# A list-scheduled attention and feed-forward kernel: new transfer figures in its planner and 82 fixed nudges of the steps' priorities

## The chip, the core and the metric

One core of a Trainium2 chip runs the kernel. The metric is device time in microseconds (us) for one execution. The engines are TensorE (PE, with its weight loads as PEld), VectorE (DVE), ScalarE (ACT), GpSimd (POOL) and SyncE (SP), whose queue issues nearly all DMA transfers.

## What is computed

Attention over 4 batches, 8 heads, 768 positions, head size 64, where each query sees the first 4 positions (sinks) and a window of 128; then a low-rank mixing over the sequence and a feed-forward pair with a residual:

```python
scores = scale * np.matmul(q, k.transpose(0, 1, 3, 2))
keep = is_sink | in_window
a = np.exp(scores - max); a = a / (np.sum(a, axis=-1, keepdims=True) + 1e-09)
x = (a @ v) as [batch, 768, 512]
u = x + (x.T @ U @ V).T          # U 768x32, V 32x768
out = u + np.maximum(u @ w_ch1, 0.0) @ w_ch2     # 512 -> 2048 -> 512
```

## The kernel before

**Tiling.** Everything is cut into tiles of 128 partitions. Attention works on a pair of heads at a time: scores of half blocks of 64 queries in 64-row tiles of PE (`scores`, line 760; "tiled" matmuls), a masked minimum on DVE (L773), the exponential on ACT (L776), the scaling by the row sums on POOL, ACT or DVE (L797, L794), transposes on PE (L815), copies with a triangular mask on ACT, DVE and POOL (L821, L823, L826), and the product with the values (L857, tiled). The mixing follows (`mix_half`, `mix_end`, L964 to L1042).

**Feed-forward.** Products are formed in a 32-bit matmul type as three products of high and low parts (hi and lo, "split" by a copy and a subtraction, L622, L623, L629, L631). Batch 0 runs plainly (`ffn`, L1077 to L1099) while the weights arrive: each piece of 64-bit weights is loaded, converted by integer steps (`narrow`, L139 to L147, tiles `nr`, `nt`, `spare`) and split into `w` tiles. The parts, and sums of quarters of them (`prepare`), are written to DRAM tensors `wd` and `ws`. Batches 1 to 3 run jointly (`ffn_joint`) with seven products of half-size blocks in place of eight (L1247), in two rounds of four pairs of blocks each; for every product a piece of 256 KB is loaded again from `wd` or `ws` into a slot of a ring (`w0` to `w5`, later `spare`), and used by 3 or 6 matmuls. The results of the products are added on DVE (L1252).

**What sets the order.** All work between the prelude and the end is first recorded as `Step` objects with an engine (or several possible ones with a cost each), reads, writes and a priority; then `Plan.order` arranges them by a list-scheduling model on the host, and the instructions are issued in that order, engine by engine. `forward` goes through time and always starts the ready step of the lowest priority value, choosing the engine of a step that can go to several; buffers of a ring and the port that DVE and POOL share are part of the model. `backward` derives new priorities from the finished plan; 40 rounds of both are run, and the plan kept whose modelled span plus that of `strained` (the same order replayed with longer steps) is least. For a DMA the model takes the issue on SP, a place in one queue of transfers (`lat`, bytes by `RATE`), and a landing after `LAND`:

```python
            if e == "SP":
                dma = max(dma, t + s.dur + 0.65 if s.dur else dma) + s.lat
                end = dma + LAND + s.slack
```

An SP instruction that waits (for a slot to be free, say) holds every later one in SP's queue. PE works off its instructions strictly in order too, so a matmul whose weights are not there stops it. The steps spoken of below are the loads of `weights` inside `ffn_joint` (recorded by `put`, L637), the masked copies of `transposes` (L821 on DVE or L823 on POOL), the conversion's last step (L146 on DVE or L147 on POOL) and the subtractions `tt` (L629 on DVE or L631 on POOL).

## Time and profile before

| | us |
|---|---|
| median of 3 runs (lowest, highest) | 682.69 (681.12, 688.5) |
| the profiled execution | 681.97 |
| its span, first to last instruction | 680.2 |
| PE busy in it | 651.1 |

The profiled execution's own time is 1.8 us more than its span. The profile is of one execution: a page of sums, and views of the trace behind it (waits by who ended them, the chain of work that ended last, groups of equal instructions, stretches of time). A busy PE includes matmuls that run slowly; its granted clock stands beside it as a share of 2.4 GHz.

### The profile page before, as it was taken

The numbers are of one execution on the slowest core, as the hardware profiler recorded it, in microseconds if no ns is written. First come the engines' busy times: TensorE is split into PE (matmuls) and PEld (weight loads), VectorE is DVE, ScalarE is ACT, GpSimd is POOL, SyncE is SP. The second block draws the span as 40 slices with busy tenths as digits, with TensorE's granted clock in tenths as the row PEclk, the third lists the DMA queues.
The fourth block names the chain that finished last, engine by engine and source line by source line (L and its number), as shares of the span: only waits on it lengthen the run. The fifth ranks groups of instructions, "written<-read, shape, count | busy, mean of one in ns | idle before, by whom it ended". The sixth has DMA issues, their size and how long they took to land.

```text
span 680.2 us, 15557 instructions
## 1 busy us (share of the span) xinstructions
PE 651.1 (96%) x5302; PEld 599.2 (88%) x5302; DVE 535.6 (79%) x1464; ACT 427.8 (63%) x1185; POOL 261.3 (38%) x336
## 2 busy tenths in 40 slices
PE   7898999999989989998999999999999999999997
PEld 5665888888979879988979989899999999999996
DVE  7999999998999878787798799666735964673483
ACT  6986788887774378774478866265437535543551
POOL 4742656357536157555144555112303211020120
PEclk9899999999999999998999999999999999999999
DMA  8569899999769799996899767968887899888882
GB/s 273 187 198 375 302 388 339 363 326 322 259 223 357 235 335 383 359 301 216 274 299 389 261 191 228 318 201 294 264 254 250 264 294 374 249 245 262 250 271 94
DMA packets 111720, 191.57 MB, mean 282 GB/s; under 512 B 10256, under 2 KB 46608, under 8 KB 111632
## 3 DMA queue, kind: packets, MB, share of 16 engines
q1 hardware_dynamic: 111200, 189.90, 83.7%
q8 instruction: 44, 0.72, 0.4%
q10 hardware_dynamic: 432, 0.59, 0.3%
q14 instruction: 44, 0.36, 0.2%
HBM read 141.17 MB, written 49.28 MB: 280 GB/s over the span
## 4 chain that ended last, share of the span: by engine, by line
PE 76%; DVE 10%; DMA 8%; ACT 2%; issue 1%; POOL 0%; SPq 0%; DVEq 0%; POOLq 0%; ACTq 0%
PE bank L1247 48%; PE bank L1099 6%; PE bank L760 4%; PE bank L857 4%; DMA w<-ws 3%; PE bank L815 3%; PE bank L1077 2%; PE bank L1079 2%; PE bank L1078 2%; DMA w<-wd 2%; DVE nt L145 1%; DVE spare L146 1%; DMA ws<-spare 1%; DVE ul L629 1%; PE bank L964 1%
## 5 line engine op out<-in xcount | busy, mean ns | idle before, releaser
L1247 PE MATMUL bank<-w,w 128*128 128x384 f32 x792 | 154.6, 339 | 3.5 <-DVE w L629 1.4
L1247 PEld LDWEIGHTS bank<-w,w 128*128 128x128 f32 x792 | 138.2, 188 | 7.1 <-DVE w L629 1.8
L776 ACT ACTIVATE p<-p,mn 128x132 f32<-128x132 f32 x192 | 75.5, 396 | 20.9 <-DVE mn L773 20.7
L1247 PE MATMUL bank<-w,spare 128*128 128x384 f32 x348 | 67.1, 338 | 0.0
L631 POOL TENSOR_TENSOR w<-uh,w 128x384 fp32r<-128x384 f32 x21 | 22.7, 1081 | 106.9 <-ACT w L622 63.7
L1252 DVE TENSOR_TENSOR big<-bank,big 128x384 f32<-128x384 f32 x84 | 44.6, 551 | 23.5 <-PE bank L1247 23.4
L1247 PEld LDWEIGHTS bank<-w,spare 128*128 128x128 f32 x348 | 61.6, 188 | 0.1
L1099 PE MATMUL bank<-w,hh 128*128 128x512 f32 x192 | 61.4, 401 | 0.0
L773 DVE CUSTOM_DVE_ANT_0 p<-bank,mask 128x132 f32<-128x132 f32 x192 | 48.4, 290 | 0.2
L1077 PE MATMUL bank<-ul,w 128*128 128x384 f32 x128 | 44.3, 346 | 4.3 <-DVE ul L629 1.7
L629 DVE TENSOR_TENSOR spare<-spare 128x128 f32<-128x128 f32 (+1 forms) x93 | 39.0, 444 | 10.1 <-DMA ws<-spare 5.8
L631 POOL TENSOR_TENSOR spare<-spare 128x128 f32<-128x128 f32 (+1 forms) x47 | 30.1, 650 | 42.2 <-DMA ws<-spare 15.8
L1247 PE MATMUL bank<-spare,w 128*128 128x384 f32 x210 | 43.0, 341 | 1.6 <-DMA w<-ws 1.6
L622 ACT CAST w<-ul 128x384 fp32r<-128x384 f32 x56 | 28.8, 514 | 24.2 <-PE bank L1247 19.0
L1079 PE MATMUL bank<-uh,w 128*128 128x384 f32 x128 | 43.1, 336 | 0.0
L1078 PE MATMUL bank<-uh,w 128*128 128x384 f32 x128 | 43.0, 336 | 0.0
L823 POOL TENSOR_SCALAR_AFFINE_SELECT oph<-oph 128x320 f32<-128x320 f32 x51 | 27.3, 548 | 36.3 <-ACT oph L622 35.6
L760 PE MATMUL bank<-kp,qp 64*64 64x196 f32 (+2 forms) x840 | 39.4, 316 | 1.5 <-DMA kp<-in_k_dram 1.3
L1099 PEld LDWEIGHTS bank<-w,hh 128*128 128x128 f32 x192 | 34.5, 188 | 6.8 <-issue 1.4
L797 POOL TENSOR_TENSOR p<-p,r 128x396 f32<-128x396 f32 x32 | 27.9, 879 | 31.4 <-DVE r L786 19.9
L826 POOL TENSOR_SCALAR_AFFINE_SELECT oph<-oph 128x384 f32<-128x384 f32 x64 | 39.6, 639 | 0.1
L1247 PEld LDWEIGHTS bank<-spare,w 128*128 128x128 f32 x210 | 36.8, 188 | 3.2 <-ACT nt L622 1.8
(284 smaller groups left out, 1658.9 us busy)
## 6 DMA issues: line engine op xcount, KB each, us to landing
w<-ws SPq DMA_DIRECT2D x132, 256.0 KB, 4.7
w<-wd SPq DMA_DIRECT2D x102, 256.0 KB, 4.2
big<-in_w_dram SPq DMA_DIRECT2D x32, 512.0 KB, 5.5
ws<-spare SPq DMA_DIRECT2D x32, 512.0 KB, 5.6
spare<-ws SPq DMA_DIRECT2D x60, 256.0 KB, 4.1
wd<-w SPq DMA_DIRECT2D x32, 384.0 KB, 5.7
spare<-wd SPq DMA_DIRECT2D x42, 256.0 KB, 3.9
vp<-in_v_dram SPq DMA_DIRECT2D x15, 384.0 KB, 5.5
```

What stands on the lines that cost most here:

```text
L629: ways = {"DVE": (dve(n), lambda: nc.vector.tensor_tensor(dst(), a(), b(), op), pool)}
L631: ways["POOL"] = (gps(n), lambda: nc.gpsimd.tensor_tensor(dst(), a(), b(), op), True)
L760: nc.tensor.matmul(st()[a * G:(a + 1) * G, x * TW + to:x * TW + to + wd], qr()[at, q0:q0 + G], kr()[at, k0:k0 + wd], start=True, stop=True ...
L773: add("DVE", dve(SW), lambda st=st, x=x, j=j, part=part, at=at: nc.vector.tensor_tensor_reduce(part(), st()[:, x * TW + half * G:x * TW + ...
L776: add("ACT", act(SW) + 0.22, lambda part=part, at=at: nc.scalar.activation(part(), part(), AF.Exp, bias=at(mn), scale=-1.0, accum_out=at(sm)),
L826: add("POOL", 0.126 + CH * 0.914e-3, lambda: nc.gpsimd.affine_select(top(), top(), [[0, NB], [1, G]], ALU.is_ge, 0.0, base=half * G, chann ...
L1077: nc.tensor.matmul(ph()[:, :CH], wh, ul()[:, c, :], start=n == 0, stop=False)
L1078: nc.tensor.matmul(ph()[:, :CH], wl, uh()[:, c, :], start=False, stop=False)
L1079: nc.tensor.matmul(ph()[:, :CH], wh, uh()[:, c, :], start=False, stop=n == NC - 1)
L1099: nc.tensor.matmul(acc[k](), a()[:, sl], w()[:, :, at, m:m + P].rearrange("p d o j -> p o d j"), start=not begin and i == 0 and j == 0, st ...
L1247: nc.tensor.matmul(bank()[:, :CH], w()[:, at:at + P], u()[:, d, :] if n > 1 else u(), start=first and i == 1, stop=last and i == 3 * n, sk ...
L1252: add("DVE", dve(CH), lambda: nc.vector.tensor_tensor(x(), bank()[:, :CH], t(), ALU.add), r=(bank,) if t is x else (bank, t), w=(x,), prio ...
```

## The change

The planner's figures are altered: a transfer lands 2.7 us after its turn in place of 1.3, moves at 360 GB/s in place of 370, and takes 0.1 us from issue to its turn in place of 0.65; issuing costs 0.55 us in place of 0.5; the surcharges on DVE steps, the price of an ACT copy and of one group of transposes are lower. After the 40 rounds, 82 seeds are applied in turn. Each picks a share of the steps, a width and a stretch of the plan, and shifts the priority of a pseudo-random part of the steps that begin there; `forward` then runs once more with the shifted priorities. The seeds are a fixed list, and nothing is tried or judged when the kernel is built. What is computed stays the same.

```diff
-LAND = 1.3
-RATE = 370e3
+LAND = 2.7
+RATE = 360e3
 BEGIN = 1.6
+ISSUE = 0.1
 SLOW = 2.0
-MORE = {"POOL": 0.05, "DVE": 0.01}
-STRAIN = {"POOL": 0.06, "DVE": 0.012, "ACT": 0.008, "SP": 0.02}
+MORE = {"POOL": 0.05, "DVE": 0.005}
+STRAIN = {"POOL": 0.06, "DVE": 0.008, "ACT": 0.008, "SP": 0.02}
+SEED = 30000000
+SHARES = ((0.02, 6), (0.1, 3), (0.5, 1), (0.005, 15))
+LENGTHS = (4, 15, 60, 700)
+MOVES = (
+    14, 21, 30, 36, 138, 157, 184, 202, 227, 304, 404, 569, 588, 647, 815, 1183, 1413, 1473, 1764,
...
+)
@@ order
         self.forward()
+        begin = [s.start for s in self.steps]
+        for move in MOVES:
+            self.nudge(SEED + move, begin)
+        self.forward()
         return sorted(self.steps, key=lambda s: (s.start, s.n))
+
+    def nudge(self, seed, begin):
+        state = (seed * 2654435761 + 12345) % 2 ** 64
+        def draw():
+            nonlocal state
+            state = (state * 6364136223846793005 + 1442695040888963407) % 2 ** 64
+            return (state >> 40) / 16777216.0
+        draw(), draw()
+        share, width = SHARES[int(draw() * 4)]
+        lo = draw() * 680 - 20
+        length = LENGTHS[int(draw() * 4)]
+        share = min(share * (700 / length) ** 0.5, 0.5)
+        for s, t in zip(self.steps, begin):
+            if (lo <= t < lo + length or length == LENGTHS[-1]) and draw() < share:
+                s.prio += (draw() + draw() + draw() - 1.5) * 2 * width
@@ strained, forward
-                dma = max(dma, free[e] + 0.65 if s.dur else dma) + s.lat
+                dma = max(dma, free[e] + ISSUE if s.dur else dma) + s.lat
@@ backward
-                p.ready_b = max(p.ready_b, s.back + p.lat + sync + (1.95 if p.eng == "SP" else 0.0) if whole else s.back - p.dur)
+                p.ready_b = max(p.ready_b, s.back + p.lat + sync + (LAND + 0.65 if p.eng == "SP" else 0.0) if whole else s.back - p.dur)
@@ copy, put, transposes
-        return self.plan.any({"ACT": (act(n) + (0.0 if psum else 0.07), lambda: nc.scalar.copy(dst(), src()), False),
+        return self.plan.any({"ACT": (act(n) + (0.0 if psum else 0.045), lambda: nc.scalar.copy(dst(), src()), False),
-        self.plan.add("SP", 0.5 if rows == P else 0.65, fn, r=r, w=((box, part),) if box else (), lat=nbytes / RATE, prio=prio).slack = slack
+        self.plan.add("SP", 0.55 if rows == P else 0.65, fn, r=r, w=((box, part),) if box else (), lat=nbytes / RATE, prio=prio).slack = slack
-        add("PE", mm(P, NBLK), mms, r=parts + [res], w=(tr,), prio=t0)
+        add("PE", 0.30, mms, r=parts + [res], w=(tr,), prio=t0)
```

Lines of the changed kernel have numbers 34 higher from `copy` on (L1247 is L1281 there, L637 is L671, L629 is L663, L631 is L665) and 12 higher before the planner (L147 is L159).

Place A is on PE, at the end of batch 1's second round of products (about 428 to 434 us in the trace); `w2` is the slot, a read of it by `spare0` is the first of a newly loaded piece. Before:

```order
L1247 MATMUL bank3_184<-w0_862,w2_1056 128x384 x3
L1247 MATMUL bank6_187<-w0_862,w3_1128 128x384 x3
L1247 MATMUL bank6_187<-w1_915,w3_1128 128x384
L1247 MATMUL bank6_187<-w0_862,w3_1128 128x384 x2
L1247 MATMUL bank6_187<-w1_915,w3_1128 128x384 x3
L1247 MATMUL bank4_185<-p2_2922,w4_1218 128x384
L1247 MATMUL bank4_185<-vp2_2884,w4_1218 128x384 x2
L1247 MATMUL bank4_185<-p2_2922,w4_1218 128x384
L1247 MATMUL bank4_185<-vp2_2884,w4_1218 128x384 x2
L1247 MATMUL bank6_187<-w1_915,w3_1128 128x384 x3
L1247 MATMUL bank1_182<-w2_1056,w5_1385 128x384 x6
L1247 MATMUL bank4_185<-spare0_3036,w2_1056 128x384 x6
```

and now, from the last read of the old piece in `w2`:

```order
L1281 MATMUL bank5_186<-w0_857,w2_1044 128x384 x3
L1281 MATMUL bank6_187<-spare0_3042,spare1_4934 128x384 x6
L1281 MATMUL bank0_181<-w1_914,w3_1093 128x384
L1281 MATMUL bank0_181<-w0_857,w3_1093 128x384 x2
L1281 MATMUL bank1_182<-w1_914,w3_1093 128x384
L1281 MATMUL bank1_182<-w0_857,w3_1093 128x384 x2
L1281 MATMUL bank0_181<-w1_914,w3_1093 128x384 x6
L1281 MATMUL bank1_182<-w1_914,w3_1093 128x384 x6
L891 MATMUL bank7_188<-oph0_5421,vp1_759 64x64
L891 MATMUL bank7_188<-oph1_5446,vp1_759 64x64
```

An attention group, 44 rows of which the first two are shown, and 16 transposes now stand between that read and the next one by `spare0`, which is 37 L1281 matmuls further on in place of 25.

Place B is in SP's queue (about 301 to 305 us in the trace): a piece of `ws1` for slot `w4`, and the loads of keys and queries for the next pair of heads, `kp1` and `qp1`. Before:

```order
L637 DMA w3_1128<-ws1_1_2597 128x512
L637 DMA kp1_85<-in_k_dram 128x792
L637 DMA qp1_86<-in_q_dram 128x768
L637 DMA w4_1218<-ws1_2_2755 128x512
L637 DMA w2_1056<-ws1_0_2122 128x512
L637 DMA w3_1128<-ws1_1_2597 128x512
L637 DMA w3_1128<-ws1_2_2755 128x512
```

and now:

```order
L671 DMA w5_1347<-ws1_3_2910 128x512
L671 DMA w2_1044<-ws1_0_2082 128x512
L671 DMA kp1_85<-in_k_dram 128x792
L671 DMA w4_1182<-ws1_2_2736 128x512
L671 DMA qp1_86<-in_q_dram 128x768
L671 DMA w3_1093<-ws1_1_2472 128x512
L671 DMA w3_1093<-ws1_2_2736 128x512
```

The load into `w4` has moved from behind `qp1` to ahead of it, and the one into `w2` ahead of `kp1`.

The third place is POOL's queue between batch 0's attention and the next one (about 55 to 110 us): joins of the conversion (`spare`) and subtractions of weights (`w`). Before:

```order
L147 TENSOR_TENSOR spare0_189<-nt_106,spare0_189 128x512
L631 TENSOR_TENSOR w1_915<-spare0_189,w1_915 128x4x128
L631 TENSOR_TENSOR ul1_975<-xT3_579,uh1_965 128x384
L147 TENSOR_TENSOR spare1_190<-nt_106,spare1_190 128x512
L631 TENSOR_TENSOR w2_1056<-spare1_190,w2_1056 128x4x128 x2
L147 TENSOR_TENSOR spare0_189<-nt_106,spare0_189 128x512 x3
L631 TENSOR_TENSOR w3_1128<-spare0_189,w3_1128 128x4x128
L631 TENSOR_TENSOR w4_1218<-spare0_189,w4_1218 128x4x128
L631 TENSOR_TENSOR vsh0_1126<-pair512a_99,vsh0_1126 32x512
L802 COPY psink_1295<-p2_1186 128x2x3x4
```

and now:

```order
L159 TENSOR_TENSOR spare0_189<-nt_106,spare0_189 128x512
L665 TENSOR_TENSOR ul0_969<-xT1_425,uh0_959 128x384
L665 TENSOR_TENSOR ul1_982<-xT1_425,uh1_967 128x384
L159 TENSOR_TENSOR spare1_190<-nt_106,spare1_190 128x512
L159 TENSOR_TENSOR spare0_189<-nt_106,spare0_189 128x512
L665 TENSOR_TENSOR w2_1044<-spare1_190,w2_1044 128x4x128
L665 TENSOR_TENSOR w3_1093<-spare0_189,w3_1093 128x4x128
L665 TENSOR_TENSOR vsh0_1131<-pair512a_99,vsh0_1131 32x512
L665 TENSOR_TENSOR w3_1093<-spare0_189,w3_1093 128x4x128
L665 TENSOR_TENSOR vsh0_1131<-pair512a_99,vsh0_1131 32x512
L836 COPY psink_1294<-p2_1184 128x2x3x4
```

Of joins there are three in place of five here, of 128x512 subtractions of weights three in place of five; the others have gone to DVE.

## Rows read from the trace of the kernel before

**Rows 1.** The page: busy us of each engine (share of the span) and instructions; granted clock in tenths.
```profile
PE 651.1 (96%) x5302; PEld 599.2 (88%) x5302; DVE 535.6 (79%) x1464; ACT 427.8 (63%) x1185; POOL 261.3 (38%) x336
...
PEclk9899999999999999998999999999999999999999
```

**Rows 2.** The chain that ended last, in order of time: start us, us, what.
```profile
302.49 7.97 DMA w<-ws
...
330.19 2.62 PE bank L964 x24
...
428.20 4.96 DMA w<-ws
...
434.59 2.28 PE bank L857 x88
...
461.74 213.38 PE bank L1247 x1218
```

**Rows 3.** Waits of PE: engine, line, waited for: us in total, times, longest us.
```profile
PE bank L1247 <- DMA w<-ws: 5.5, 4, 2.3
...
PE bank L815 <- POOL p L797: 2.4, 2, 2.1
...
PE bank L1077 <- DVE hl L1088: 1.7, 1, 1.7
...
PE bank L1247 <- DMA w<-wd: 1.7, 2, 1.0
...
PE bank L1247 <- DVE w L629: 1.4, 1, 1.4
```

**Rows 4.** Timeline of PE: start us, us, instructions, [idle before, what ended it].
```profile
310.60 0.77 PE L1247 MATMUL bank<-hh,w 128*128 128x384 f32 x3 [2.33 <-DMA w<-ws]
...
416.70 0.76 PE L1247 MATMUL bank<-w,w 128*128 128x384 f32 x3 [0.92 <-DMA w<-ws]
...
433.30 1.29 PE L1247 MATMUL bank<-spare,w 128*128 128x384 f32 x6 [1.55 <-DMA w<-ws]
```

**Rows 5.** Windows: us; busy us (instructions) by engine; granted clock, DMA share, GB/s.
```profile
8.00:62.00 54.00, 46.16 (x506) 34.39 (x506) 50.51 (x204) 47.62 (x173) 27.45 (x46) 0.97 0.74 251
62.00:234.00 172.00, 167.69 (x1343) 146.38 (x1344) 162.90 (x415) 123.53 (x321) 90.12 (x102) 1.00 0.92 316
306.00:308.00 2.00, 2.00 (x13) 1.83 (x11) 2.00 (x6) 1.99 (x6) 1.75 (x3) 1.00 1.02 406
310.00:312.00 2.00, 1.40 (x10) 1.40 (x11) 0.36 (x1) 0.27 (x1) 0.00 (x0) 0.96 0.84 312
312.00:314.00 2.00, 2.00 (x11) 1.91 (x10) 0.56 (x1) 0.87 (x3) 1.72 (x4) 0.50 0.05 17
314.00:316.00 2.00, 2.00 (x10) 2.00 (x9) 0.67 (x2) 0.82 (x3) 0.16 (x1) 0.69 0.05 8
```

**Rows 6.** DMA issues: out<-in, queue, count, KB each, median us from issue to landing.
```profile
w<-ws SPq DMA_DIRECT2D x132, 256.0 KB, 4.7
```

**Rows 7.** Groups by line, 8 to 62 us, then 62 to 234: count, busy us, mean ns, idle before.
```profile
L145 DVE SCALAR_TENSOR_TENSOR nt<-big,nr 128x512 uint16<-128x512 uint16 x4 | 3.0, 741 | 0.2
...
L821 DVE TENSOR_TENSOR oph<-bank,tri 128x320 f32<-128x320 f32 x5 | 2.3, 478 | 0.0
...
L145 DVE SCALAR_TENSOR_TENSOR nt<-big,nr 128x512 uint16<-128x512 uint16 x28 | 27.1, 974 | 0.5 <-ACT nr L144 0.5
...
L146 DVE TENSOR_TENSOR spare<-nt,spare 128x512 uint16<-128x512 uint16 x20 | 17.4, 880 | 0.1
...
L629 DVE TENSOR_TENSOR w<-spare,w 128x512 fp32r<-128x512 f32 x12 | 9.3, 792 | 0.1
...
L631 POOL TENSOR_TENSOR w<-spare,w 128x512 fp32r<-128x512 f32 x17 | 23.2, 1368 | 14.0 <-ACT w L622 12.9 <-DVE w L623 0.6 <-POOL vsh L631 0.5
...
L147 POOL TENSOR_TENSOR spare<-nt,spare 128x512 int32<-128x512 int32 x8 | 11.9, 1487 | 16.4 <-DVE nt L145 16.4
```

More of the change, by code (lines that the diff above doesn't have):

```diff
@@ L500, in forward @@
             if e == "SP":
-                dma = max(dma, t + s.dur + 0.65 if s.dur else dma) + s.lat
+                dma = max(dma, t + s.dur + ISSUE if s.dur else dma) + s.lat
                 end = dma + LAND + s.slack
```

5 rows, old and new, of the table MOVES are left out of this document.

## The prediction

> **What bounds the kernel now.** First the page's busy shares: PE is busy 651.1 of 680.2 us, DVE 535.6, POOL 261.3 [rows 1]. PE is the bound on the average; whatever the change can win lies in PE's 29.1 idle us and in stretches where PE runs slowly. Second, the chain of waits: its last piece is 213.38 us of 1218 matmuls of line 1247 without a break, so nothing is to be won after 461 us, and one such matmul costs 213.38/1218 = 0.175 us [rows 2]. Before that the same view runs through loads of weights (`w<-ws`), two of which stand in the rows. Third, the list of waits of PE: 5.5 us in four waits for `w<-ws`, 1.7 us in two for `w<-wd`, 7.2 us together; 1.7 us for `hl` and 1.4 us for `w`, both made by DVE; 2.4 us in the opening for POOL's scaling, before transposes of line 815 [rows 3]. The timeline of PE gives the three longest of the waits for loads, 2.33, 1.55 and 0.92 us [rows 4]. Fourth, windows: from 62 to 234 us PE is busy 167.69 of 172.00 us and DVE 162.90, so there two engines are nearly full; before that (8 to 62 us) DVE is busy 50.51 of 54.00 [rows 5].
>
> So the profile has three parts: an opening on DVE, a first feed-forward part on PE and DVE together, and a middle part (234 to 461 us) where PE waits above all for transfers. The end is closed.
>
> **The change, part by part.** It alters no instruction's size: 4200 matmuls before and after, 630 DMAs of SP, and the same 80 alternations between tiled and whole matmuls. It changes the order, and which of two engines does some elementwise steps.
>
> *Loads that land late.* The old figures let a load of 256 KB land 0.65 + 0.71 + 1.3 = 2.7 us after its issue (262144 / 370e3 = 0.71); the new ones 0.1 + 0.73 + 2.7 = 3.5 us. The trace's median is 4.7 us [rows 6]. I call lead the PE work that stands in the order between the matmul that frees a load's slot and the first matmul that reads the load; with the wait added it is what the load needed.
> Place A, the end of batch 1's last round: in the old order 24 matmuls of line 1247 stand between the last read of `w2` and the next read of a new load in it, 24 x 0.175 = 4.2 us. The load took 4.96 us from issue to landing [rows 2], and PE waited 1.55 us [rows 4]. In the new order 36 such matmuls, an attention group (2.28 us) and 16 transposes (2.62/24 = 0.109 us each) stand there [rows 2]: 6.3 + 2.28 + 1.7 = 10.3 us, more than the 4.2 + 1.55 = 5.75 that were needed. A neighbour had a lead of 4.7 and a wait of 0.92 us [rows 4]; loads in that round now have at least 5.0, most 5.8 or more. Of 2.47 us I take 2.2 as gone.
> Place B, the load issued at 302.49 us: it took 7.97 us [rows 2] because the queue was full (DMA share 1.02, 406 GB/s, [rows 5]); PE waited 2.33 us [rows 4]. Its lead hardly changes (30 matmuls and 6 transposes before, 24 and 15 now: 5.9 and 5.8 us). But SP issues it ahead of a 384 KB load of `qp`, not behind it; at 406 GB/s that is 0.97 us. I take 1.0 us.
> The other three waits together are 7.2 - 2.33 - 1.55 - 0.92 = 2.4 us. The leads of their loads go from 6.2 to at least 7.1, from 7.4 to 11.2, and from 5.3 to 5.6 us: of 0.8 us each I take 0.5, 0.7 and 0.3, 1.5 us, as gone.
> Sum -4.7 us; bounds 0 (all waits come back elsewhere) and -7.2 (none comes back).
>
> *The clock.* After the wait of place B the granted clock falls to its lower level, 1.2 GHz: 0.96, 0.50 and 0.69 in three rows of 2 us [rows 5], which is 0.08 + 1.00 + 0.62 = 1.7 us lost. After the waits of 1.55 us and 1.7 us it stayed up, for no other slice past the opening is under 9 [rows 1]. With about 1.3 us left at place B it should stay up: -1.7 us, bounds 0 and -1.7.
>
> *Two waits for DVE* (1.7 us for `hl` in the first feed-forward part, 1.4 us for `w` in the middle part, [rows 3]). Both places are ordered anew, and DVE is fuller at the first. I take -1.0; bounds 0 and -3.1.
>
> *The opening.* Counted on the order, DVE has 183 steps ahead of the first feed-forward matmul in place of 176: four more masked copies of line 821, which POOL's line 823 did before, and three more short steps of the weights' conversion. 4 x 0.478 [rows 7] is 1.9 us, with three at half that price 2.6 us. DVE's idle time from 8 to 62 us is 54.00 - 50.51 = 3.5 us [rows 5], so it may swallow them; ACT has five steps fewer. And POOL's copies stood in the queue of the scaling that PE waited for (2.4 us, [rows 3]). I take +1.0; bounds -2 and +2.7.
>
> *The first feed-forward part.* From there up to the last matmul of line 1077 DVE gets 379 steps in place of 354, POOL 89 in place of 98. Seven subtractions of 128x512 (792 ns each) and three joins of line 146 (880 ns) make 5.5 + 2.6 = 8.1 us; fifteen others, at some 0.3 us each as an estimate between these and the conversion's short steps, bring it to some 12 us [rows 7]. POOL loses six of 1368 ns and four of 1487 ns [rows 7], 14 us, and gets a few short ones: 13 us less. DVE's steps are longer where POOL works: line 145 takes 974 ns here and 741 ns in the opening [rows 7], 28 x 0.233 = 6.5 us. POOL's 90.12 us [rows 5] fall by 13, so at least 1 us of that comes back, and up to 6.5 if the long steps are those that go; I take 4 over all kinds. Net +8 us of DVE work against 172.00 - 162.90 = 9.1 us of DVE idle time [rows 5]. It just fits, and the steps are moved forward in time, not added: over the whole kernel DVE does 17 more. I take 0; bounds -2 (work done early is not waited for later) and +8.
> The Trainium skill says (SBUF — State Buffer, Who interferes with whom) that DVE and GpSimd share one pair of ports as an exclusive lock, so that one blocks the other for a whole instruction. By that rule work taken from POOL frees DVE, which is the direction of the 741 and 974 ns. By it alone the term would be nearer -2 than +8; I keep 0, for DVE's own added work is the larger number.
>
> *New short waits.* 9 loads keep leads of 5.0 to 6.0 us (16 before), and in the last part, where the least lead was 8.4 us, three have 5.8 or 6.3; the median need there is about 4 us, hence no cost if the queue is as full as now, up to 1 us each if not. One transpose (line 934) now stands directly behind the one whose copy delays its own input on ACT. Together +1.2; bounds 0 and +5.
>
> **Sum.** -4.7 - 1.7 - 1.0 + 1.0 + 0 + 1.2 = -5.2 us. The profiled execution took 681.97 us, so 676.8; the median of the runs shown, 682.69, is 0.7 above it and one run in three is 688.5. I say 677.
>
> **Rivals.**
> *Everything pays (about 669).* All six waits and the clock go (-8.9), the DVE waits too (-3.1), and the opening does not lengthen: 681.97 - 12 = 670, and 669 with 1 us from the opening. For it: place A's lead more than doubles, and in the middle part no lead is under 5.0 us. Against: place B's lead does not grow.
> *The waits come back (about 681).* The loads need 8 us where the queue is full, whatever is planned, and bytes are the same; only place A pays (-2.2) and the opening costs 1.0. 681.97 - 2.2 + 1.0 = 680.8. For it: leads of 5 to 6 us against needs of 5.7 to 8.2.
> The Trainium skill gives a single transfer as 2.0 us plus bytes / 436e3 (DMA: Bandwidth & Descriptors, Anatomy of one DMA, for GpSimd's path): an estimate of 2.6 us for 256 KB. By that rule the old figure of 2.7 was right and the waits are those of a queue, as this rival has it, with its 681. The median of 4.7 us [rows 6] and the 4.96 us of place A [rows 2] differ from it, and the measurement decides.
> *DVE becomes the bound (about 688, slower).* In the first feed-forward part DVE's +8 us find no idle time, since its 9.1 us are in part waits for ACT, PE and DMA; the opening costs its full 2.7. It decides as soon as DVE's work up to the last matmul of line 1077 passes the 172 us that PE takes: 162.9 + 12 - 4 = 170.9, so 1 us away, or at once where POOL's relief fails. With no relief, 0.3 of the idle time of use, and the loads and the clock still paying (4.7 + 1.7): 681.97 + 2.7 + 12 - 2.7 - 6.4 = 687.6. Against it: the planner sees DVE's queue and the shared port.
>
> **How the numbers follow.** Forecast 0.47, everything pays 0.20, waits come back 0.20, DVE bound 0.13. A measurement of this kernel tells about 1% from no change (6.8 us, so 675.9 and 689.5 are the edges). Faster: all of the first rival and 0.2 of the forecast's spread (673 to 681), 0.40. Slower: under half of the last rival, and a little for new waits beyond their bound, 0.08. The rest is 0.52. The range 669 to 686 takes in the first two rivals and about half of the last.
>
> **What would show it.** Right: PE's waits for `w<-ws` and `w<-wd` fall from 7.2 to under 3.5 us; no row of half clock near 312 us; place A without a wait; the first matmul of line 1077 within 2 us of where it was, the last part again without a gap. Wrong: DVE at over 98% between 62 and 234 us with PE waits for `w`, `ul` or `hl` of over 6 us; or waits for loads of 5 us and more at new places.

## The result and the profile after

The changed kernel takes 671.38 us (four runs, 670.65 to 671.74) where the kernel before takes 681.90 on the same chip: a ratio of 0.9864, with a 95% interval of 0.9818 to 0.9909. That is 1.4% faster. The forecast was 677 with a range of 669 to 686; the gain of 10.5 us is twice the 5.2 forecast, and nearer to the rival "everything pays". The profiled execution went from 681.97 to 671.74 us, its span from 680.2 to 670.0.

The page's busy times and clock, to set beside [rows 1], and its costliest group (339 ns is the mean time of one matmul from its start to its end; ends are modelled, and matmuls overlap). L1111 is line 1077 of before, L1133 line 1099, L849 line 815, L891 line 857 and L998 line 964:

```profile
PE 648.8 (97%) x5302; PEld 599.0 (89%) x5302; DVE 527.9 (79%) x1481; ACT 426.6 (64%) x1186; POOL 248.6 (37%) x320
...
PEclk8999999999999999999999999999999999999999
...
L1281 PE MATMUL bank<-w,w 128*128 128x384 f32 x792 | 156.6, 339 | 1.3 <-DMA w<-ws 1.3
```

PE's idle time falls from 680.2 - 651.1 = 29.1 to 670.0 - 648.8 = 21.2 us, and its busy time by 2.3. Together that is the 10.2 us of the span. The windows tell in which part of the program. The columns are those of [rows 5]; first the row of the kernel before that was not shown yet, the middle part:

```profile
234.00:461.00 227.00, 217.50 (x2178) 199.71 (x2177) 185.31 (x572) 151.64 (x474) 101.73 (x140) 0.99 0.86 287
```

and the three windows of the changed kernel:

```profile
8.00:62.00 54.00, 45.58 (x520) 34.47 (x515) 51.03 (x215) 45.22 (x166) 25.70 (x43) 0.97 0.76 255
62.00:234.00 172.00, 169.35 (x1356) 146.66 (x1358) 160.02 (x428) 125.69 (x331) 78.25 (x94) 1.00 0.93 322
234.00:461.00 227.00, 224.51 (x2240) 209.89 (x2231) 184.71 (x585) 155.11 (x484) 101.24 (x133) 1.00 0.89 295
```

Idle time of PE in the opening: 7.84 before, 8.42 now. In the first feed-forward part: 4.31 and 2.65. In the middle part: 9.50 and 2.49, which is 7.0 of the 7.9 us. Two more readings place the gain there: the 128th matmul of line 1077 starts at 233.4 us before and 236.2 now, while the window from 62 to 234 us holds 13 more matmuls, so that part is nearly where it was; the last closed stretch of line 1247 began at 461.74 us [rows 2] and begins now at 451.83.

The waits of PE in the changed kernel, to set beside [rows 3]:

```profile
PE bank L849 <- POOL p L831: 3.9, 4, 1.9
PE bank L1074 <- DVE t L1061: 2.7, 1, 2.7
PE bank L1281 <- DMA w<-ws: 1.6, 2, 1.3
...
PE bank L1133 <- DVE hl L1122: 1.1, 1, 1.1
PE bank L1022 <- DVE xhl L663: 0.8, 2, 0.6
PE bank L981 <- DVE pst L663: 0.8, 1, 0.8
```

Loads of weights cost 1.6 us here and, in one more row, 0.3 us for `spare<-ws`: 1.9 in place of 7.2. The timeline shows all of what is left of them in the middle part (start, us, instructions, in brackets the idle time before and what ended it):

```profile
306.21 0.77 PE L1281 MATMUL bank<-hh,w 128*128 128x384 f32 x3 [0.31 <-DMA w<-ws]
...
352.19 1.29 PE L1281 MATMUL bank<-w,w 128*128 128x384 f32 x6 [1.28 <-DMA w<-ws]
```

The first is place B: 0.31 us in place of 2.33 [rows 4]. The second is a new place. The chain of waits shows the two loads, and place A without any (start, us, what):

```profile
300.09 5.99 DMA w<-ws
...
344.07 7.98 DMA w<-ws
...
422.51 2.28 PE bank L891 x88
424.78 2.31 PE bank L1281 x12
427.09 1.75 PE bank L998 x16
...
451.83 93.20 PE bank L1281 x531
545.03 4.91 DMA spare<-ws
```

The load of place B landed 5.99 us after its issue, not 7.97; its lead had not grown. At place A the attention group (88 matmuls) and the 16 transposes stand where the forecast counted them, and no load stands in the chain between 352 and 545 us. The load of 7.98 us, now at 344 us, shows that the full queue has not gone: its long landing has moved to a load with another lead.

### The profile page after: what moved, and what is told of

It reads as the page before. It is cut to its first block, busy times and chain, and to the rows that moved or that the text cites. A ratio compares the mean times of both kernels' runs of the same rounds, so it can differ in the third digit from the quotient of the medians.

```text
span 670.0 us, 15532 instructions
## 1 busy us (share of the span) xinstructions
PE 648.8 (97%) x5302; PEld 599.0 (89%) x5302; DVE 527.9 (79%) x1481; ACT 426.6 (64%) x1186; POOL 248.6 (37%) x320
## 4 chain that ended last, share of the span: by engine, by line
PE 78%; DVE 14%; DMA 4%; issue 1%; ACT 1%; POOL 1%; POOLq 0%; SPq 0%; DVEq 0%; ACTq 0%
PE bank L1281 51%; PE bank L1133 7%; PE bank L891 4%; PE bank L794 4%; PE bank L849 2%; PE bank L1111 2%; PE bank L1113 2%; PE bank L1112 2%; DMA w<-ws 2%; DVE nt L157 1%; DVE p L807 1%; DVE spare L158 1%; DVE w L663 1%; DVE nr L154 1%; DVE spare L663 1%
## 5 line engine op out<-in xcount | busy, mean ns | idle before, releaser
L1281 PE MATMUL bank<-w,w 128*128 128x384 f32 x792 | 156.6, 339 | 1.3 <-DMA w<-ws 1.3
L1281 PEld LDWEIGHTS bank<-w,w 128*128 128x128 f32 x792 | 138.3, 188 | 3.9 <-issue 1.8
L1281 PE MATMUL bank<-w,spare 128*128 128x384 f32 x348 | 68.0, 338 | 0.0
L1281 PEld LDWEIGHTS bank<-w,spare 128*128 128x128 f32 x348 | 61.6, 188 | 0.3 <-DVE w L663 0.2
L1133 PE MATMUL bank<-w,hh 128*128 128x512 f32 x192 | 61.3, 400 | 0.0
L665 POOL TENSOR_TENSOR w<-uh,w 128x384 fp32r<-128x384 f32 x18 | 19.9, 1106 | 74.2 <-ACT w L656 63.5
L1111 PE MATMUL bank<-ul,w 128*128 128x384 f32 x128 | 44.5, 347 | 0.7 <-POOL ul L665 0.6
L656 ACT CAST w<-ul 128x384 fp32r<-128x384 f32 x57 | 29.1, 513 | 24.7 <-PE bank L1281 21.5
L1281 PE MATMUL bank<-spare,w 128*128 128x384 f32 x210 | 42.1, 339 | 0.0
L665 POOL TENSOR_TENSOR spare<-spare 128x128 f32<-128x128 f32 (+1 forms) x43 | 29.8, 706 | 32.6 <-DMA ws<-spare 11.4
L794 PE MATMUL bank<-kp,qp 64*64 64x196 f32 (+3 forms) x840 | 39.9, 324 | 1.4 <-DMA kp<-in_k_dram 1.4
L1133 PEld LDWEIGHTS bank<-w,hh 128*128 128x128 f32 x192 | 34.8, 188 | 6.4 <-issue 2.0
L663 DVE TENSOR_TENSOR spare<-spare 128x128 f32<-128x128 f32 (+1 forms) x97 | 38.1, 418 | 1.9 <-ACT spare L656 1.3
L1133 PE MATMUL bank<-w,hl 128*128 128x512 f32 x96 | 38.1, 397 | 1.1 <-DVE hl L1122 1.1
L831 POOL TENSOR_TENSOR p<-p,r 128x396 f32<-128x396 f32 x30 | 26.5, 890 | 31.1 <-DVE r L820 26.3
L891 PEld LDWEIGHTS bank<-oph,vp 128*64 128x64 f32 (+1 forms) x1200 | 33.7, 136 | 4.6 <-issue 2.0
```

The lines of the kernel that those rows point to most:

```text
L663: ways = {"DVE": (dve(n), lambda: nc.vector.tensor_tensor(dst(), a(), b(), op), pool)}
L665: ways["POOL"] = (gps(n), lambda: nc.gpsimd.tensor_tensor(dst(), a(), b(), op), True)
L794: nc.tensor.matmul(st()[a * G:(a + 1) * G, x * TW + to:x * TW + to + wd], qr()[at, q0:q0 + G], kr()[at, k0:k0 + wd], start=True, stop=True ...
L891: nc.tensor.matmul(pa()[i * D:(i + 1) * D, c:c + (hi - lo) * G], vr()[at, i, kb, :], mv, start=pa not in begun, stop=last, skip_group_chec ...
L1111: nc.tensor.matmul(ph()[:, :CH], wh, ul()[:, c, :], start=n == 0, stop=False)
L1133: nc.tensor.matmul(acc[k](), a()[:, sl], w()[:, :, at, m:m + P].rearrange("p d o j -> p o d j"), start=not begin and i == 0 and j == 0, st ...
```

## The experiments

All ratios are to the kernel before, timed on the same chip in the same session: figures_only to nudges_old_figures in one session, half_nudges with the small loads and before_pool_twice in a second, the three landing times with other_nudges in a third. The median of the kernel before was 683.3 to 683.5 us in each of them. A ratio need not be that of two medians: for figures_only it is as if before took 667.45 / 0.9825 = 679.3 us. "Leads" are counted on the order as in the prediction. A table of the readings first, from each run's own times, waits and windows ("first" is the start of the first matmul of line 1077; "rest" is the profile's span from there to its end; "idle" is PE's idle time from 234 to 461 us):

| kernel | us | ratio (95%) | waits for loads of weights, us | first, us | rest, us | idle, us |
|---|---|---|---|---|---|---|
| before | 681.97 (profiled) | 1 | 7.2 | 62.6 | 617.6 | 9.50 |
| changed | 671.38 | 0.9864 (0.9818 to 0.9909) | 1.9 | 63.3 | 606.7 | 2.49 |
| figures_only | 667.45 | 0.9825 (0.9778 to 0.9871) | none | 61.9 | 603.4 | 1.73 |
| landing_only | 673.06 | 0.9884 (0.9854 to 0.9914) | none | 66.7 | 604.1 | 2.19 |
| rest_only | 681.50 | 0.9994 (0.9954 to 1.0034) | 5.4 | 60.9 | 618.3 | 8.24 |
| nudges_old_figures | 689.03 | 1.0163 (1.0086 to 1.0241) | 6.0 | 65.2 | 621.4 | 7.58 |
| half_nudges | 673.79 | 0.9876 (0.9841 to 0.9910) | 1.1 | 62.8 | 608.8 | 3.24 |
| other_nudges | 703.95 | 1.0299 (1.0238 to 1.0361) | 2.0 | 68.7 | 635.8 | 4.26 |
| figures_land13 | 672.85 | 0.9847 (0.9789 to 0.9904) | 2.7 | 60.1 | 611.5 | 5.08 |
| figures_land35 | 669.63 | 0.9802 (0.9746 to 0.9859) | none | 64.3 | 603.7 | 1.49 |
| figures_land43 | 673.49 | 0.9861 (0.9804 to 0.9918) | none | 65.2 | 606.1 | 2.39 |
| before_small_loads | 671.54 | 0.9836 (0.9799 to 0.9873) | none | 63.4 | 607.1 | 1.92 |
| after_small_loads | 669.82 | 0.9813 (0.9780 to 0.9847) | none | 65.4 | 604.1 | 0.86 |
| before_pool_twice | 696.53 | 1.0207 (1.0157 to 1.0257) | 5.1 | 65.8 | 630.2 | 7.43 |

**Which part of the change pays: figures or nudges.** Four kernels. The first keeps the new figures and drops the nudges:

```diff
-MOVES = (14, 21, 30, ...
+MOVES = ()
```

> The new figures, all of them, without the 82 nudges. Counted on the order, loads of the joint part have leads of at least 6.4 us up to its 370th matmul, but for one stretch (480th to 710th) with 4.6, 5.1 and 5.6; 5 of 115 are under 6 us (before 16, after the change 9). Theory 'leads' (the 10 us of the change are the waits for loads in the middle part, with the clock that falls behind the longest, and longer leads take them away whoever made them): PE waits for w<-ws and w<-wd under 2.5 us in all (7.2 before), no half clock in the middle, and 671 to 675 us. Rival 'search' (the gain is that of the nudges, picked one by one over the whole program, and the figures only move waits about): 677 to 682 us. Rival 'elementwise' (the gain is DVE's and POOL's division of work): POOL has 345 steps here, 9 more than before and 25 more than after, so 680 us or more.

Measured: 667.45 us, no wait for `w<-ws` or `w<-wd`, a granted clock of 9 tenths in every slice. These are all of PE's waits of 0.2 us and more for anything between 234 and 670 us (lines are 7 lower than in the changed kernel):

```profile
PE bank L974 <- DVE xT L977: 1.0, 1, 1.0
PE bank L842 <- DVE xT L1069: 0.7, 1, 0.7
```

No load is among them. It is 3.5 us faster than the least that theory "leads" expected (671 to 675), and its median is 3.9 us under the changed kernel's. "Search" and "elementwise" fall, the latter because POOL does more here (345 steps) than in either kernel. What puts it below its range is not in the middle part, where PE's idle time is only 0.8 us less than in the changed kernel. In the first feed-forward part PE idles 172.00 - 171.18 = 0.8 us in place of 2.65, and the granted clock from 8 to 62 us is 1.00 in place of 0.97, which is 1.6 us:

```profile
8.00:62.00 54.00, 45.22 (x523) 33.88 (x517) 51.65 (x214) 45.99 (x170) 28.10 (x45) 1.00 0.77 262
62.00:234.00 172.00, 171.18 (x1393) 148.38 (x1394) 163.56 (x433) 125.53 (x330) 79.54 (x96) 1.00 0.95 323
```

The second adds the transfer figures alone to the kernel before:

```diff
-LAND = 1.3
-RATE = 370e3
+LAND = 2.7
+RATE = 360e3
+ISSUE = 0.1
...
-        self.plan.add("SP", 0.5 if rows == P else 0.65, fn, ...
+        self.plan.add("SP", 0.55 if rows == P else 0.65, fn, ...
```

> The kernel before with the new figures of transfers alone (landing, rate, issue), the prices of the engines as they were, no nudges. 9 of 116 leads of the middle part are under 6 us, the least 4.9. Theory 'leads': as many under 6 us as after the change, so waits for loads of 1.5 to 3.5 us in place of 7.2 and 672 to 676 us. Rival 'search': 677 to 683 us.

Measured: 673.06 us, in the expected range, with no wait for loads at all (1.5 to 3.5 us were expected). Its opening is 4.1 us longer than before's (66.7 against 62.6). From there to the end it takes 604.1 us in place of 617.6, 13.5 less, and so about as long as with all the new figures (603.4).

The third takes the other figures alone:

```diff
-MORE = {"POOL": 0.05, "DVE": 0.01}
+MORE = {"POOL": 0.05, "DVE": 0.005}
...
-        add("PE", mm(P, NBLK), mms, r=parts + [res], w=(tr,), prio=t0)
+        add("PE", 0.30, mms, r=parts + [res], w=(tr,), prio=t0)
```

> The kernel before with the other new figures alone (the surcharges of DVE, the price of a copy, 0.30 us for three transposes), the figures of transfers as they were, no nudges. 18 of 118 leads of the middle part are under 6 us, 7 under 5, the least 3.7. Theory 'leads': nothing gained, waits for loads of 7 to 11 us, 681 to 688 us. Rival 'elementwise': these are the figures that divide DVE's and POOL's work, so a good part of the gain is here: 673 to 677 us.

Measured: 681.50 us, nothing gained. Waits for loads are 5.4 us, a little under the 7 to 11 expected, though more of its leads are under 6 us than before's (18 against 16). So the count of short leads does not give the microseconds, nor does it order the kernels: other_nudges below has 16 of them and 2.0 us of waits, landing_only 9 and none, figures_land13 8 and 2.7.

The fourth puts the 82 nudges on the plan of the old figures:

> The same 82 nudges on the plan of the old figures. 16 of 115 leads of the middle part are under 6 us, 8 under 5, the least 3.3, and in the last part five are from 3.7 to 5.2 us (before none under 8.4). Theory 'leads': slower than before, waits for loads of 9 to 15 us, some of them in the last part, 684 to 694 us. Rival 'search' (the nudges themselves are good): 672 to 680 us.

Measured: 689.03 us. The time is in the expected range, the waits are not: 6.0 us in place of 9 to 15, of which 1.8, 1.2, 0.7 and 0.3 us stand in the last part, where before had none. Part of its loss is elsewhere: its opening is 2.6 us longer. So the direction came out as the theory has it, and only part of the size by its mechanism.

**What the loads are worth, with the order left alone.** In both kernels' orders the loads of weights of the joint part move 64 KB in place of 256 KB:

```diff
-        self.put(piece, lambda: (f32(piece()).rearrange(...), f32(view())), 1 << 18, prio, r=(box,))
+        self.put(piece, lambda: (f32(piece()).rearrange(...)[:, 0, :P], f32(view())[:, 0, :P]), 1 << 18, ...
...
-                        nc.tensor.matmul(bank()[:, :CH], w()[:, at:at + P], ...
+                        nc.tensor.matmul(bank()[:, :CH], w()[:, 0:P], ...
```

> The order of the kernel before, unchanged, but each load of weights of the joint part moves the first 128 of its 512 columns (64 KB in place of 256 KB), and line 1247 multiplies by these columns alone: the rest of those weights is left out. Theory 'leads': the loads now land within the leads they have, so the waits for w<-ws and w<-wd (7.2 us), the half clock behind one of them (1.7 us) and some 0.1 us of restart at each go: 672 to 675 us, the order of before at nearly the time of the changed kernel. Rival 'elementwise' (PE would have waited at the same places for DVE, ACT or POOL a little later): 677 to 682 us, with new waits for w, ul or hl in the middle part.

> The order of the changed kernel, unchanged, with the same small loads (columns 128 to 511 of those weights are left out). Theory 'leads': only 1.9 us of waits for loads are left there, so 668.5 to 670.5 us; with the run of the order of before, the two orders then differ by 3 to 5 us in place of 10 to 12. Rival 'elementwise': the two orders still differ by 8 us or more.

Measured: 671.54 us, just under its expected range, and 669.82, within it. The order of before, untouched, reaches the time of the changed kernel once its loads are small: 683.27 - 671.54 = 11.7 us by the medians of that session, 680.2 - 670.5 = 9.7 by the spans of the two profiles. The two orders then differ by 1.7 us, less than the 3 to 5 expected. The middle part of before with small loads, its loads in the list of DMA issues (KB each, median us from issue to landing), and the start of its closed end in the chain:

```profile
234.00:461.00 227.00, 225.08 (x2247) 210.81 (x2246) 189.11 (x585) 158.07 (x486) 103.86 (x141) 1.00 0.57 179
...
w<-ws SPq DMA_DIRECT2D x132, 64.0 KB, 2.0
...
452.08 213.36 PE bank L1247 x1218
```

PE is busy 225.08 of 227 us, against 217.50 in before and 224.51 in the changed kernel, at a granted clock of 1.00 and 179 GB/s of DMA traffic in place of 287. The order is the same, so the stretch from the 128th matmul of line 1077 to the closed end can be set beside that of before: 452.08 - 235.83 = 216.3 us in place of 461.74 - 233.44 = 228.3, 12.0 us less. So the loads are most of the gain. With small loads the difference of the two orders falls from 10.5 to 1.7 us by the medians, and from 10.9 to 3.0 us by the profiles from the first matmul of line 1077 on (607.1 and 604.1); what is left is the order's own. The run has one limit: smaller loads also relieve every other transfer, so these figures are the price of the loads with their queue, not of their leads alone.

**How the nudges cost.** The first 41 of the 82, and 82 others:

```diff
-        for move in MOVES:
+        for move in MOVES[:41]:
```

> The new figures with the first 41 of the 82 nudges. The figures alone took 667.45 us, with all 82 nudges 671.38. 8 of 116 leads of the middle part are under 6 us (none of the nudges 5, all of them 9), the last part has the short leads of 5.8 us already. If nudges cost time evenly as they wear the leads down: 668 to 671 us. If a few early nudges do it: 671 to 673. If the harm is in the second half alone: 666 to 668.

```diff
-SEED = 30000000
+SEED = 60000000
```

> The new figures with 82 other nudges: the same numbers on another seed, so that nothing picked them. 16 of 111 leads of the middle part are under 6 us, the least 3.0, and 13 fewer... the last part has leads from 4.2 us. If picking is worth something on the chip: 676 to 686 us, well above the 671.38 of the picked ones, with waits for loads of 3 us or more. If any shake of the order costs the same 4 us: 670 to 674 us.

Measured: 673.79 us with the first 41, above every case that the expectation had, and 703.95 us with the unpicked 82, far above theirs. Neither is explained by loads: the waits for them are 1.1 and 2.0 us. The unpicked nudges lose in the first feed-forward part, and in the last part PE waits for steps of DVE:

```profile
PE bank L1281 <- DVE w L663: 3.8, 4, 1.4
PE bank L1111 <- DVE ul L663: 2.1, 1, 2.1
PE bank L1281 <- DVE hh L663: 1.9, 1, 1.9
...
62.00:234.00 172.00, 163.72 (x1293) 139.16 (x1293) 161.59 (x436) 122.25 (x320) 73.67 (x85) 0.98 0.91 313
```

PE does 1293 matmuls in these 172 us where the changed kernel does 1356. A part of the loss is the clock: the mean granted clock over the span of this profile is 0.983, in the changed kernel 0.996, which is 12.0 against 2.7 us of full clock. So the nudges that were kept are some 32 us better than this other list of 82, the only one that was run, yet the best of these kernels has none. Between none and all 82 the medians differ by 3.9 us and the runs do not overlap (666.99 to 669.01 and 670.65 to 671.74), but they were timed in different sessions and the intervals of the ratios overlap, so a loss is likely and not settled. What the profiles show of it: 1.9 us of waits for loads that the figures alone don't have, 1.8 us more idle time of PE from 62 to 234 us, and an opening 1.4 us longer, which is within what one execution differs from another (*The opening*, below).

**How much landing time.** The new figures without nudges, with one number changed:

```diff
-LAND = 2.7
+LAND = 1.3
```

(3.5 and 4.3 in the other two.)

> The new figures without nudges, but the landing time put back from 2.7 to 1.3 us (rate, issue and engines' prices stay new). 8 of 117 leads of the middle part are under 6 us, 4 under 5, the least 3.3. Theory 'leads' (the landing time is what lengthens the leads): waits for loads of 3 to 7 us come back, 673 to 680 us, against 667.45 with 2.7. Rival (the other figures do it): 667 to 670 us.

> The new figures without nudges, the landing time raised from 2.7 to 3.5 us. 3 of 112 leads of the middle part are under 6 us, the least 5.4. Theory 'leads': no wait for a load is left to take away (none stands in the list of waits of the figures alone), so 666 to 670 us. Rival 'more is better': under 665. Rival 'too long costs' (steps ahead of the loads are held up): over 671.

> The same with 4.3 us, so that a load of 256 KB counts 5.1 us, above the 4.7 of the trace of before. No lead of the middle part is under 6 us, the least is 6.3. Theory 'leads': 666 to 671 us, no wait for w<-ws or w<-wd over 0.3 us. Rival 'too long costs': over 671 with waits for DVE or ACT in their place.

Measured: 672.85, 669.63 and 673.49 us. These three were timed together, and their executions do not overlap: 3.5 (669.40 to 669.84) is 3 to 4 us faster than 1.3 and 4.3. The 667.45 at 2.7 is of another session, and by the ratios it cannot be told from any of the three. At 1.3 loads are waited for again (1.9 and 0.8 us, a little under the expected 3), and PE idles 5.08 us in the middle part in place of 1.73 at 2.7. At 3.5 and 4.3 no load is waited for and the middle part is about as full as at 2.7, but at 4.3 the third reading comes true, "too long costs", with POOL's scaling waited for more than DVE or ACT: 6.0 us in place of 4.1. The opening is 3.3 us longer than at 2.7; the granted clock there (0.97 against 1.00 from 8 to 62 us) makes 1.6 of it. At 4.3:

```profile
PE bank L842 <- POOL p L824: 6.0, 5, 2.0
PE bank L991 <- DVE xT L977: 1.8, 1, 1.8
PE bank L974 <- DVE pst L656: 1.7, 1, 1.7
```

So of the four values, without nudges, only 1.3 leaves waits for loads, and the three above it shift the other waits. From the first matmul of line 1077 on the four take 611.5, 603.4, 603.7 and 606.1 us. Each value gives one plan, so that a difference of a few us may also be the luck of one order; that rival was not tested. The 1.3 us row also says that the landing time is not the whole of it: with the other new figures the old value gives 672.85, without them the other figures alone 681.50. Which of rate, issue and the cost on SP makes up that rest was not tried.

**What POOL's work costs DVE.** In the kernel before, POOL's 17 subtractions of 128x512 are issued twice, with the order unchanged:

```diff
-ways["POOL"] = (gps(n), lambda: nc.gpsimd.tensor_tensor(dst(), a(), b(), op), True)
+ways["POOL"] = (gps(n), lambda: [nc.gpsimd.tensor_tensor(dst(), a(), b(), op) for _ in range(2 if again else 1)], True)
```

> The order of before, with each of POOL's 17 subtractions of 128x512 weights in the first feed-forward part issued twice (the same result written again): 17 x 1.37 = 23 us more of POOL's work between 62 and 234 us, none on DVE. Theory 'shared port' (work that leaves POOL gives DVE back much of its time, which the forecast took at 4 us for 13): line 145 lengthens from 974 to over 1050 ns and DVE's busy time between 62 and 234 us grows by 4 to 10 us. Rival (DVE's long steps have another cause): line 145 within 950 to 1000 ns and DVE's busy time within 2 us of 162.90.

The run is slower throughout, so the same work (1343 matmuls, 416 instructions of DVE) stands from 65 to 253 us. Its window, its groups of DVE and POOL there (count, busy us, mean ns), PE's longest wait there, and last line 142 of the kernel before:

```profile
65.00:253.00 188.00, 176.12 (x1343) 152.53 (x1344) 172.02 (x416) 123.56 (x321) 115.71 (x119) 0.95 0.85 289
...
L631 POOL TENSOR_TENSOR w<-spare,w 128x512 fp32r<-128x512 f32 x34 | 47.5, 1400 | 13.5 <-ACT w L622 11.4 <-POOL vsh L631 0.7
L145 DVE SCALAR_TENSOR_TENSOR nt<-big,nr 128x512 uint16<-128x512 uint16 x28 | 26.1, 939 | 0.5 <-ACT nr L144 0.5
L146 DVE TENSOR_TENSOR spare<-nt,spare 128x512 uint16<-128x512 uint16 x20 | 18.4, 933 | 0.1
L142 DVE TENSOR_SCALAR nr<-nr 128x512 bf16<-128x512 bf16 x28 | 16.3, 595 | 0.0
...
PE bank L815 <- POOL p L797: 3.7, 1, 3.7
...
L142 DVE TENSOR_SCALAR nr<-nr 128x512 bf16<-128x512 bf16 x28 | 12.3, 452 | 0.6 <-ACT nr L140 0.6
```

DVE's busy time rises from 162.90 [rows 5] to 172.02, 9.1 us, for POOL's 115.71 - 90.12 = 25.6 us. "Shared port" has the sum right, and the line wrong: line 145 stays at 939 ns (974 before), line 146 goes from 880 to 933, and line 142 from 452 (12.3 us) to 595 ns. Which steps lengthen is a matter of what they stand beside, as the start and end times of single steps show. In the kernel before, the 13 steps of line 142 that lie beside no step of POOL last 285 ns on the mean, the 11 that lie beside one for at least half of their time 712; with the doubled work there are 16 of the latter kind. For line 145 it is 743 ns (17 steps) and 1525 ns (7 steps). The kernel is 13 us slower, more than DVE's 9, and the rows show what else came. PE's idle time in the window is 188.00 - 176.12 = 11.9 us where [rows 5] have 4.3, 3.7 of it one wait for POOL's scaling; and the granted clock is 0.95 in place of 1.00, some 9 us of full clock. How these shares overlap was not measured, and this kernel was timed only twice (695.25 and 697.80 us).

## Why the prediction was right, and where its numbers failed

*What bounds the kernel.* Right: PE is the bound, its last part stayed closed but for one wait of 0.3 us, and the gain lies in PE's idle time and its clock before 461 us. (The page counts 5302 matmuls in both kernels, not 4200; nothing rests on that number.)

*Loads.* The forecast was -4.7 of 7.2 us for the six old waits; they lost 6.9 (0.31 is left at place B). Place A went as counted. The steps that were too small are "I take 1.0 us" for place B, where 2.0 went, since the load landed in 5.99 us in place of 7.97, and the shares of the other three waits, "I take 0.5, 0.7 and 0.3", where all 2.4 us went. The landing of place B, 2 us earlier, was not counted ahead. The sum also lacked a term. By the page a matmul of line 1281 lasts 339 ns from its start to its end on the mean, and one follows the other at 93.20/531 = 0.175 us in the chain's closed row. So a wait costs, by this estimate, 339 - 175 = 164 ns more than its idle time, while the matmul before it runs out, which counts as busy. Ten waits of over 0.15 us in the middle part became three, 7 x 0.164 = 1.1 us. With small loads the 12.0 us of the order of before are then 7.2 for the waits, 1.7 for the clock and 1.1 for this; the other 2.0 us are not accounted for.

*The clock.* Right in sign and size: with 0.3 us left at place B the granted clock of the middle part is 1.00, and PE's busy time falls by 2.3 us, of which 1.7 were forecast for the clock; the 1.1 us just estimated, which count as busy, are the likely rest.

*Waits for DVE.* Of the two that were counted, `w` went and 1.1 of 1.7 us are left for `hl`: -2.1 where -1.0 was taken. The term left out the smaller waits. The largest of them stands in the list of before:

```profile
PE bank L1077 <- DVE ul L629: 1.7, 2, 1.2
```

1.2 us of it come before the first matmul of line 1077, so in the opening, and 0.5 behind it. From that matmul to 461 us all waits for DVE of over 0.15 us are 5.4 us before (0.75 for `xT`, 0.54 for `ul`, 0.16, 0.20, 1.71, 0.34, 0.23 and 1.44) and 2.8 now (1.08 for `hl`, 0.26 and 0.59 for `xhl`, 0.85 for `pst`): -2.6. No experiment took these waits apart, but the size is near the 3.0 us by which the two orders still differ with small loads.

*The opening.* Forecast +1.0, measured +0.7 (62.6 to 63.3). The two runs with small loads have the same opening as their originals (no load of the joint part is issued before 208 us) and start line 1077 at 63.4 and 65.4 us. So one execution differs from the next by up to 2 us there, and the term cannot be told from nothing. The clock is a part of it: from 8 to 62 us it is 0.95 and 0.93 in these two, 0.97 in both originals.

*The first feed-forward part.* The time was right (forecast 0; PE's idle time fell by 1.7 us), the working only in half. Priced by the mean times of before, DVE's added steps between the first and the 128th matmul of line 1077 are 12.2 us, the 12 that were counted. But "I take 4" for the relief of the port was far too small: DVE's busy time between these two matmuls went from 161.7 to 160.9 us, so 13 us came back for POOL's 11.6 less (10.8 of them by the mean times of the groups that both have). The largest part stands in one line:

```profile
L157 DVE SCALAR_TENSOR_TENSOR nt<-big,nr 128x512 uint16<-128x512 uint16 x28 | 21.3, 774 | 0.0
```

28 steps at 774 ns in place of 974 [rows 7], 5.6 us; the prediction's upper bound of 6.5 us was for this line. Now 20 of the 28 steps lie beside no step of POOL and 5 beside one for half their time or more, where it was 17 and 7. The run with POOL's work doubled gives 0.36 us of DVE for one of POOL, close to the 4 for 13 that was taken, and the change itself gave about 1. So no single ratio holds: which of DVE's steps stand beside POOL's decides. By the Trainium skill (SBUF — State Buffer, Who interferes with whom) DVE and GpSimd share a pair of ports as an exclusive lock. The trace agrees with the direction in both runs (285 and 712 ns for line 142); the section gives neither size.

*New waits.* Forecast +1.2, measured 1.6 for two new waits for loads (1.28 and 0.3 us).

*The terms together.* Measured they are -6.9 for the old loads, +1.6 for the new, -1.7 for the clock, -1.1 for the run-out, -2.6 for DVE and +0.7 for the opening: -10.0, beside -10.2 us by the spans. The forecast of -5.2 had the path right, PE waiting for loads, and was half the size: it was 2.2 us short for the old loads, 1.6 for DVE, 1.1 for the run-out that it lacked. Its caution of taking only part of each wait failed for the loads and for DVE alike. That the measured terms come out so near is in part luck, as the opening alone varies by 2 us.

*The rivals.* "Everything pays", at 669, had the mechanism right for the loads: the six waits (but for 0.31 us) and the clock went, and its "against" (place B's lead does not grow) was no obstacle, since the load landed earlier. Its time is near as well. "The waits come back" falls: its ground was that loads need 8 us where the queue is full whatever is planned. One load still needed 7.98 us, but only 1.28 of it were waited for. "DVE becomes the bound" falls by the relief above. The small loads of 64 KB take a median of 2.0 us from issue to landing, those of 256 KB 4.7 before, 4.3 now and 4.1 with the figures alone. The Trainium skill's figure for one transfer on GpSimd's path (DMA: Bandwidth & Descriptors, Anatomy of one DMA), 2.0 us plus bytes / 436e3, gives an estimate of 2.15 us for the first, which agrees, and of 2.6 for the second, which does not. A plan that counts 3.5 us for the large ones, as the figures alone do, left no waits; one that counts 2.7, as before, left 7.2 us of them.

## What to carry to other kernels

Where a planner orders transfers, the figure for a transfer should come from the trace under load, and is best tried from both sides. Too short, and the bound engine waits for loads: 2.7 us of waits at a landing time of 1.3, none at 2.7, 3.5 and 4.3. Too long, and the waits move to other engines: 673.49 us at 4.3 against 669.63 at 3.5. Count leads in microseconds of the bound engine's own work between the freeing of a slot and its next use, and set them beside the landing times of the trace. That told that place A's wait would go. It did not tell place B's, where the lead stayed and the load landed 2 us earlier, and the number of short leads did not give the waits. A list of nudges should be tested on the chip against the plan that it starts from: here the plan without the 82 nudges had the lowest median of all, 667.45 us, though its gain over the plan with them is likely and not settled.

## What was not expected of the hardware

The granted clock does not follow the length of the one wait before it. In the run of the other figures alone it fell after a wait of 2.20 us (a shorter one of 0.66 us followed):

```profile
68.15 0.50 PE L1099 MATMUL bank<-w,hh 128*128 128x512 f32 x1 [2.20 <-ACT w L622]
...
70.00:72.00 2.00, 2.00 (x6) 1.51 (x6) 2.00 (x5) 0.23 (x2) 0.00 (x0) 0.50 1.04 411
```

In the changed kernel it fell after one of 1.91 us and did not fall after one of 2.73 us:

```profile
13.14 1.71 PE L849 MATMUL bank<-ident,p 128*128 128x128 f32 x6 [1.91 <-POOL p L831]
...
12.00:16.00 4.00, 2.79 (x26) 2.00 (x30) 2.55 (x20) 4.00 (x19) 3.20 (x5) 0.67 0.98 329
...
58.48 0.44 PE L1074 MATMUL bank<-vst,t 128*128 128x384 f32 x1 [2.73 <-DVE t L1061]
...
58.00:60.00 2.00, 1.52 (x9) 1.52 (x10) 1.94 (x5) 1.02 (x2) 0.23 (x1) 1.00 1.03 364
```

A clock of 0.67 over 4 us stands behind the shorter wait and 1.00 behind the longer one; 0.50 is the lower level, 1.2 GHz. So in these rows a wait of about 2 us cost another 1 to 2 us or nothing, and only the rows of the run itself tell which. Executions of one kernel differ along with it: on the chip of the first session the kernel before took 677.70 us at a mean granted clock of 0.997 and 686.31 us at 0.987, where 0.010 of 680 us would be 6.8 of the 8.6 us between them.
